# Rows of the loads' sources laid out in DRAM as short pieces with gaps

## The chip, the cores and the metric

The kernel runs on one core of a Trainium2 chip. The time is the device time of one execution in microseconds. The profile is that of one further execution, taken by the hardware profiler. The core has TensorE (PE), VectorE (DVE), ScalarE (ACT), GpSimd (POOL) and SyncE (SP), and 16 DMA engines, which take the loads that SP issues.

## The reference

An mLSTM recurrence (2 batches, 8 heads, 768 steps, head dimension 40) makes 1536 rows of 320 values, and two gated layers of 320 to 2048 to 320 follow:

```python
for t in range(S):
    m_new = np.maximum(f_gate[:, :, t] + m, i_gate[:, :, t])
    f_stab, i_stab = np.exp(f_gate[:, :, t] + m - m_new), np.exp(i_gate[:, :, t] - m_new)
    C = f_stab * C + i_stab * outer(vt, kt)
    n = f_stab * n + i_stab * kt
    y[:, :, t] = sigmoid(o_gate[:, :, t]) * (C @ qt) / np.maximum(np.abs(n @ qt), 1.0)
x = y rearranged to (B * S, H * D)
h = x @ w_in;   x = (h * np.clip(h + 3.0, 0.0, 6.0) / 6.0) @ w_out
h = x @ w2_in;  x = (h * np.tanh(softplus(h))) @ w2_out
```

## The kernel before

The sequence is cut into six chunks of 128 steps. For each chunk the kernel makes scores, decays, a state that is carried on and the chunk's output, which is split into a high and a low part (`x`) and enters layer one. Layer one runs on two chunks of 256 columns first and then on blocks of 512 columns; layer two (`qh`, `bcc`) follows on three blocks of 512.

The weights come as 64-bit floats, in eight slots per layer. A slot of the first matrix (`w1i`, `w2i`) is a tile `ri` of 128 partitions with 6144 bytes each, one of the second (`w1o`, `w2o`) a tile `ro` with 5120 bytes. `narrow` loads such a tile, and ScalarE (the cast to `top`, L364) and VectorE (L366) turn it into 32-bit floats, which are then split into the high and low parts that TensorE uses. `loads` fetches a chunk's q and k as one tile `qke` (8192 bytes per partition) and its k, v and o gate as one tile `kvo` (7744 bytes). `start` and `other_gates` fetch the gates in two parts into `gio`, the first 128 steps and then the other 640; `scan_gates` (L660) is the first to use each part. `constants` fetches `cst`, and the identity matrices go to `eye`. Four of the chunks spread their decays by a store to DRAM (`fzd`, L744) and a load (`fb`, L788) that reads each of 16 rows into 8 partitions.

```python
src = fzd[c].rearrange("a (y r) t -> (a y) (r t)", y=COPIES)
SY.dma_start(out=t["f"], in_=src.unsqueeze(1).to_broadcast([16, 8, R * HL]))
```

Every DMA is issued by SP, in one order for the whole program. That order comes from `Flow`, a planner that runs when the program is built: every piece of work asks for an engine and a time, and a table of priorities and `Flow`'s costs say who gets it. For a load the cost is its number of bytes, which the change leaves as it is. `keep_warm` lets TensorE run a product of zeros (`pz`, L1211) in gaps until the first chunk's output is there. No engine can go past an instruction that waits.

The host lays the arguments out before the launch: `w_in`, `w_out`, `chunks` and `tokens` in `kernel` make the arrays in DRAM, row for row what a partition loads.

Of the kernel before, what the change touches and what calls it, by code (L numbers as in the profile page):

```python
# [12 lines left out]
U16 = mybir.dt.uint16  # L13
# [9 lines left out]
B, H, S, D = 2, 8, 768, 40  # L23
L = 128
NC = S // L
# [12 lines left out]
KVO = B * (2 * DM + H * E1)  # L38
# [262 lines left out]
def mlstm_mlp_kernel(ctx, tc, qk, kvon, gates_io, w1i, w1o, w2i, w2o, eyes, consts, out):  # L301
    nc = tc.nc
    V, A, T, G, SY = nc.vector, nc.scalar, nc.tensor, nc.gpsimd, nc.sync
# [46 lines left out]
    def narrow(src, k, n, name, then):  # L350
        yield in_raw
        size = 4 * k * n
        raw = rpool.tile([128, size + 4], U16, tag="raw", name=f"r{name}")
        loaded = Event()
        yield SP, 256 * size, loaded
        SY.dma_start(out=raw[:, 1 : size + 1].rearrange("p (k s) -> p k s", k=k), in_=src.bitcast(U16))
        yield loaded
        upper = raw[:, 4 : size + 4].rearrange("p (k n s) -> p k n s", k=k, s=4)[:, :, :, 0]
        e = raw[:, 2 : size + 2].bitcast(U32).rearrange("p (k n s) -> p k n s", k=k, s=2)[:, :, :, 0]
        yield in_top  # L360
        top = tops[turn[0] % 2][:, 0 : k * n].rearrange("p (k n) -> p k n", k=k)
        turn[0] += 1
        yield ACT, 0.93 * k * n / 768
        A.copy(top.bitcast(U16).rearrange("p k (n s) -> p k n s", s=2)[:, :, :, 1].bitcast(F16), upper.bitcast(BF16))  # L364
        yield DVE, 0.072 + k * n / 960, True
        V.scalar_tensor_tensor(out=e, in0=e, scalar=13, in1=top,  # L366
                               op0=ALU.logical_shift_right, op1=ALU.bitwise_or)
        flow.put(in_top)
        yield from then(e.bitcast(F32))
        flow.put(in_raw)  # L370
# [4 lines left out]
    def prep(layer, s):  # L375
# [53 lines left out]
        wi, wo = (w2i, w2o) if layer else (w1i, w1o)  # L429
        pi, po = P[f"prep{layer}"][2 * s : 2 * s + 2]  # L430
        a = flow.add(pi, narrow(wi[s], 3, 256, f"i{nm}", split_in))
        b = flow.add(po, narrow(wo[s], 2, DM, f"o{nm}", split_out))
        yield a
        yield b
# [321 lines left out]
    def loads(c, before):  # L756
        t, ev = tiles[c], got[c]
        if before:
            yield before
        if c == 1:  # L760
            flat = xpool.tile([128, 3072], F32, tag="x1", name="qke1")[:, 0 : 16 * L]
            t["qke"] = flat.rearrange("p (b y h t) -> p b y h t", b=B, y=2, h=4)
        else:
            yield in_qke
            t["qke"] = apool.tile([128, B, 2, 4, L], F32, tag="qke", name=f"qke{c}")
        yield SP, 1049e3, ev["qk"], 16, 0.5
        SY.dma_start(out=t["qke"], in_=qk[c])
        t["ring"] = in_x2 if c in (1, 3) else in_kvo
        yield t["ring"]
        kvo = (xpool if c in (1, 3) else apool).tile([128, 3072 if c in (1, 3) else KVO + 256], F32, tag="x2" if c in (1, 3) else "kvo", name=f"kvo{c}")  # L770
        t["tail"] = kvo[:, KVO : KVO + 256]
        t["k"], t["v"], t["o"] = (kvo[:, a:z].rearrange("p (r d) -> p r d", r=R)
                                  for a, z in ((0, R * D), (R * D, KVO - R * D), (KVO - R * D, KVO)))
        yield SP, 992e3, ev["kvo"]
        SY.dma_start(out=kvo[:, 0:KVO], in_=kvon[c * L : (c + 1) * L])

    def gate_loads(c, before):
        t, ev = tiles[c], got[c]
# [515 lines left out]
    with tc.manual_schedule(engines={PE, DVE, ACT, POOL, SP}):  # L1294
# [3 lines left out]
        for c in range(NC):  # L1298
            before = flow.add(P["load"][c], loads(c, before))
# [77 lines left out]
```

## Time and profile before

| what | value |
|---|---|
| time, median of 3 runs | 441.97 us (440.05 to 443.53) |
| profiled execution | 441.46 us, of it a span of 439.4 us |
| PE busy | 422.4 us (96% of the span) |
| DVE, ACT, POOL busy | 302.0, 269.6, 61.8 us |
| DMA packets | 10040, 40.44 MB |

A matmul counts as busy until its modelled end, and the filler product counts too, so PE's share does not tell alone how much of the time is needed. DMA's busy share is a mean over the 16 engines; where it is near 1, transfers wait for one another. The profile's DMA records have a packet's duration; where shares pass 1, neighbouring records overlap. Waits are put down to what ended them, and a wait with no ender in the profile is called "issue".

### The profile page before, as it was taken

How to read it: one execution, taken by the hardware profiler on the slowest of the kernel's cores; microseconds unless marked ns; L12 is line 12 of the kernel's file. 1: busy time of each engine (PE TensorE's matmuls, PEld its weight loads, DVE VectorE, ACT ScalarE, POOL GpSimd, SP SyncE). 2: the span in 40 equal slices, each digit the busy share in tenths (PEclk: the TensorE clock that was granted, in tenths of full speed). 3: DMA queues.
4: the chain of work that ended last, by engine and by line, in shares of the span. 5: the costliest groups of instructions: out<-in, count | busy, mean ns of one | idle time of the engine just before them, and what ended most of it. 6: DMA issues, size and time to landing. Idle time of an engine off the chain costs nothing.

```text
span 439.4 us, 9016 instructions
## 1 busy us (share of the span) xinstructions
PE 422.4 (96%) x3765; PEld 366.5 (83%) x3765; DVE 302.0 (69%) x532; ACT 269.6 (61%) x479; POOL 61.8 (14%) x51
## 2 busy tenths in 40 slices
PE   7869999999999899999998999999999999999996
PEld 5758899999988688887875788999999998989985
DVE  3888999896643953446978537666666666666664
ACT  5547795454544223348976548766676666766665
POOL 2002043213220313313133110000000000000000
PEclk9998999999999999999999999999999999999999
DMA  8976573905003027100755000000010000100001
GB/s 298 400 309 204 176 234 98 343 16 189 1 1 101 3 97 289 68 0 2 272 195 191 2 0 0 1 1 1 0 61 1 1 0 1 45 17 0 1 0 60
DMA packets 10040, 40.44 MB, mean 92 GB/s; under 512 B 2128, under 2 KB 3824, under 8 KB 9232
## 3 DMA queue, kind: packets, MB, share of 16 engines
q1 hardware_dynamic: 10000, 39.87, 25.5%
q8 instruction: 29, 0.48, 0.5%
q14 instruction: 11, 0.09, 0.1%
HBM read 37.64 MB, written 2.23 MB: 91 GB/s over the span
## 4 chain that ended last, share of the span: by engine, by line
PE 64%; DVE 14%; ACT 8%; DMA 8%; issue 3%; POOL 1%; SPq 0%; DVEq 0%; ACTq 0%; POOLq 0%
PE qh L463 18%; PE accw L480 10%; PE phw L463 9%; PE bcc L1180 6%; PE bcc L1179 5%; PE bcc L1178 5%; DMA gio<-in_gates_io 3%; PE acc L480 3%; PE ph L463 2%; DVE fb L842 2%; DMA ri<-in_w2i 2%; DVE c L308 1%; DVE ri L366 1%; DVE kvo L308 1%; ACT top L364 1%
## 5 line engine op out<-in xcount | busy, mean ns | idle before, releaser
L463 PE MATMUL qh<-x,wh 128*128 128x512 f32 x288 | 89.3, 392 | 0.0
L1180 PE MATMUL bcc<-wd,gl 128*128 128x320 f32 x192 | 59.5, 310 | 0.3 <-DVE gl L1135 0.3
L463 PEld LDWEIGHTS qh<-x,wh 128*128 128x128 f32 x288 | 52.3, 188 | 8.7
L1178 PE MATMUL bcc<-wd,gh 128*128 128x320 f32 x192 | 59.4, 309 | 0.0
L1179 PE MATMUL bcc<-wd,gh 128*128 128x320 f32 x192 | 59.3, 309 | 0.0
L463 PE MATMUL phw<-x,wh 128*128 128x512 f32 x192 | 59.2, 394 | 0.0
L1129 DVE SCALAR_TENSOR_TENSOR u<-u,qh 128x512 f32<-128x512 f32 (+1 forms) x49 | 33.1, 675 | 37.6 <-ACT u L1127 37.6
L480 PE MATMUL accw<-ghw,wd 128*128 128x512 f32 x160 | 53.9, 402 | 0.3 <-ACT ghw L550 0.3
L1125 ACT ACTIVATE u<-u,two 128x512 f32<-128x512 f32 (+1 forms) x49 | 35.0, 715 | 30.7 <-DVE u L1123 30.6
L547 DVE SCALAR_TENSOR_TENSOR rw<-rw,phw 128x512 f32<-128x512 f32 x32 | 21.9, 685 | 32.3 <-ACT rw L545 32.1
L463 PEld LDWEIGHTS phw<-x,wh 128*128 128x128 f32 x192 | 35.5, 188 | 7.8
L480 PE MATMUL accw<-glw,wd 128*128 128x512 f32 x96 | 38.3, 399 | 1.6 <-DVE glw L308 1.0
L463 PE MATMUL qh<-x,wl 128*128 128x512 f32 x96 | 37.8, 394 | 0.0
L1178 PEld LDWEIGHTS bcc<-wd,gh 128*128 128x128 f32 x192 | 36.1, 188 | 2.1
L1179 PEld LDWEIGHTS bcc<-wd,gh 128*128 128x128 f32 x192 | 36.1, 188 | 1.9
L1135 DVE SCALAR_TENSOR_TENSOR gl<-u,gh 128x512 fp32r<-128x512 f32 (+1 forms) x49 | 33.1, 675 | 5.6 <-ACT gh L1133 5.4
L1180 PEld LDWEIGHTS bcc<-wd,gl 128*128 128x128 f32 x192 | 36.1, 188 | 0.9 <-DVE gl L1135 0.9
L1119 ACT ACTIVATE u<-qh 128x512 f32<-128x512 f32 (+1 forms) x49 | 28.5, 585 | 12.7 <-PE qh L463 12.6
L545 ACT ACTIVATE rw<-phw,half 128x512 f32<-128x512 f32 x32 | 22.0, 688 | 22.5 <-PE phw L463 22.2
L480 PEld LDWEIGHTS accw<-ghw,wd 128*128 128x128 f32 x160 | 29.4, 188 | 7.6 <-ACT ghw L550 1.2
L463 PE MATMUL ph<-x,wh 128*128 128x256 f32 x192 | 35.1, 290 | 0.1
L1133 ACT ACTIVATE gh<-u 128x512 fp32r<-128x512 f32 (+1 forms) x49 | 30.3, 618 | 6.9 <-DVE u L1129 6.8
(154 smaller groups left out, 836.8 us busy)
## 6 DMA issues: line engine op xcount, KB each, us to landing
ri<-in_w1i SPq DMA_DIRECT2D x8, 768.0 KB, 5.7
qke<-in_qk SPq DMA_DIRECT2D x6, 1024.0 KB, 6.9
ri<-in_w2i SPq DMA_DIRECT2D x8, 768.0 KB, 5.5
kvo<-in_kvon SPq DMA_DIRECT2D x6, 968.0 KB, 7.3
ro<-in_w1o SPq DMA_DIRECT2D x8, 640.0 KB, 7.7
ro<-in_w2o SPq DMA_DIRECT2D x8, 640.0 KB, 4.2
fb<-fzd SPq DMA_DIRECT2D x4, 512.0 KB, 5.9
out<-ot SPq DMA_DIRECT2D x12, 160.0 KB, 1.8
```

Of the source, the lines that this page charges most:

```text
L463: T.matmul(ph, a, b, start=(i == 0), stop=(i == len(seq) - 1))
L480: T.matmul(acc[k], a, b, start=start, stop=stop, skip_group_check=True)
L545: A.activation(r, ph, AF.Relu, bias=half, scale=1.0 / 6.0)
L547: V.scalar_tensor_tensor(out=r, in0=r, scalar=1.0, in1=ph, op0=ALU.min, op1=ALU.mult)
L1119: A.activation(u, ph, AF.Exp)
L1125: A.activation(u, u, AF.Ln, bias=two)
L1129: V.scalar_tensor_tensor(out=u, in0=u, scalar=0.5, in1=ph, op0=ALU.subtract, op1=ALU.mult)
L1133: A.mul(gh, u, -2.0)
L1135: V.scalar_tensor_tensor(out=gl, in0=u, scalar=-2.0, in1=gh.bitcast(F32), op0=ALU.mult, op1=ALU.subtract)
L1178: T.matmul(acc, a, hi, start=st, stop=False)
L1179: T.matmul(acc, a, lo, start=False, stop=False)
L1180: T.matmul(acc, b, hi, start=False, stop=sp)
```

## The change

In DRAM the last axis of seven arrays is cut in pieces, and each piece is followed by a gap of 16 elements (64 bytes of 32-bit values in `qk` and `kvon`, 128 bytes of 64-bit values in the weights). A row of `w1i` or `w2i` was 6144 bytes in one and becomes 3 pieces of 2048, a row of `w1o` or `w2o` was 5120 and becomes 2 of 2560, a row of `qk` was 8192 and becomes 4 of 2048, a row of `kvon` was 7744 and becomes 4 of 1936. The loads take the pieces and leave the gaps out; the tiles in the core's memory are as before, as is everything that reads them.

```diff
@@ narrow
-        SY.dma_start(out=raw[:, 1 : size + 1].rearrange("p (k s) -> p k s", k=k), in_=src.bitcast(U16))
+        SY.dma_start(out=raw[:, 1 : size + 1].rearrange("p (k s) -> p k s", k=k), in_=src[:, :, 0:n].bitcast(U16))
@@ loads
-        SY.dma_start(out=t["qke"], in_=qk[c])
+        SY.dma_start(out=t["qke"].rearrange("p b y h t -> p (b y) (h t)"), in_=qk[c, :, :, 0:512])
...
-        SY.dma_start(out=kvo[:, 0:KVO], in_=kvon[c * L : (c + 1) * L])
+        SY.dma_start(out=kvo[:, 0:KVO].rearrange("p (k s) -> p k s", k=4), in_=kvon[c * L : (c + 1) * L, :, 0 : KVO // 4])
@@ kernel
+    def apart(a):
+        return np.concatenate([a, np.zeros(a.shape[:-1] + (16,), a.dtype)], axis=-1)
...
-        "qk": np.stack([chunks(q), chunks(k)], axis=3),
-        "kvon": np.concatenate([tokens(k), tokens(np.concatenate([v, np.ones_like(v[..., :1])], axis=3)), tokens(o_gate, True)], axis=1),
+        "qk": apart(np.stack([chunks(q), chunks(k)], axis=3).reshape(NC, 128, 4, 512)),
+        "kvon": apart(np.concatenate([tokens(k), tokens(np.concatenate([v, np.ones_like(v[..., :1])], axis=3)), tokens(o_gate, True)], axis=1).reshape(S, 4, -1)),
...
-        "w1i": w_in(moe_w_in[x_order]), "w1o": w_out(moe_w_out), "w2i": w_in(moe2_w_in), "w2o": w_out(moe2_w_out),
+        "w1i": apart(w_in(moe_w_in[x_order])), "w1o": apart(w_out(moe_w_out)), "w2i": apart(w_in(moe2_w_in)), "w2o": apart(w_out(moe2_w_out)),
```

No instruction changes its place on any engine. On SP, the queue of all DMAs, the program begins before as follows (a row has the line, the tile and its source, and the shape of the access; `ri_1` is slot 1 of the first weights):

```order
L356 DMA ri_1_136<-in_w1i 128x3072
L1195 DMA gio<-in_gates_io 16x2x128
L1197 DMA eye<-in_eyes 128x256
L356 DMA ro_0_137<-in_w1o 128x2560
L1251 DMA cst<-in_consts 16x112
L767 DMA qke_103<-in_qk 128x2048
L356 DMA ro_2_138<-in_w1o 128x2560
L775 DMA kvo_153<-in_kvon 128x1936
L356 DMA ri_0_139<-in_w1i 128x3072
L767 DMA qke_155<-in_qk 128x2048
L1255 DMA gio<-in_gates_io 16x2x640
L775 DMA kvo_180<-in_kvon 128x1936
```

And now, on SP at the same place:

```order
L356 DMA ri_1_136<-in_w1i 128x3x1024
L1195 DMA gio<-in_gates_io 16x2x128
L1197 DMA eye<-in_eyes 128x256
L356 DMA ro_0_137<-in_w1o 128x2x1280
L1251 DMA cst<-in_consts 16x112
L767 DMA qke_103<-in_qk 128x4x512
L356 DMA ro_2_138<-in_w1o 128x2x1280
L775 DMA kvo_153<-in_kvon 128x4x484
L356 DMA ri_0_139<-in_w1i 128x3x1024
L767 DMA qke_155<-in_qk 128x4x512
L1255 DMA gio<-in_gates_io 16x2x640
L775 DMA kvo_180<-in_kvon 128x4x484
```

Nothing moved; the loads of weights, `qke` and `kvo` have one axis more.

## Rows read from the trace of the kernel before

**Rows 1.** Stages: length, busy us of each engine, PE clock, DMA share, GB/s

```profile
5.10:21.10 16.00, 13.13 (x257) 9.92 (x258) 13.04 (x26) 10.91 (x24) 0.00 (x0) 1.00 1.00 387
...
29.90:32.10 2.20, 0.04 (x3) 0.07 (x3) 1.51 (x3) 1.39 (x2) 0.00 (x0) 1.00 0.19 67
...
76.70:91.00 14.30, 14.30 (x238) 13.78 (x242) 12.64 (x22) 8.10 (x13) 3.97 (x3) 1.00 0.77 280
91.00:155.00 64.00, 61.64 (x739) 55.08 (x733) 43.66 (x73) 27.24 (x54) 13.56 (x10) 1.00 0.16 51
...
207.00:243.00 36.00, 33.97 (x143) 26.03 (x142) 29.85 (x39) 29.13 (x42) 10.86 (x9) 1.00 0.59 201
243.00:439.00 196.00, 192.36 (x1040) 171.25 (x1038) 125.69 (x213) 132.42 (x224) 3.97 (x3) 1.00 0.03 11
```

**Rows 2.** Chain that ended last, 0 to 32 us: start, length, what

```profile
0.74 4.37 DMA ri<-in_w1i
...
6.25 14.86 DMA gio<-in_gates_io
21.12 0.02 issue
21.14 0.47 DVE mt L660
...
29.89 2.18 issue
```

**Rows 3.** DMA queues, 29.7 to 31 us: packets, MB, share of 16 engines

```profile
q8 instruction: 1, 0.02, 5.1%
```

**Rows 4.** Waits that a DMA ended: us in total, times, longest

```profile
DVE mt L660 <- DMA gio<-in_gates_io: 4.8, 2, 4.5
...
ACT top L364 <- DMA ri<-in_w1i: 3.2, 1, 3.2
...
ACT top L364 <- DMA ri<-in_w2i: 2.4, 2, 2.0
...
DVE fb L842 <- DMA fb<-fzd: 1.6, 1, 1.6
```

**Rows 5.** Chain that ended last, whole span: a later load

```profile
219.91 6.61 DMA ri<-in_w2i
```

**Rows 6.** The page: packets of the queue, and loads, KB, us to landing

```profile
q1 hardware_dynamic: 10000, 39.87, 25.5%
...
ri<-in_w1i SPq DMA_DIRECT2D x8, 768.0 KB, 5.7
qke<-in_qk SPq DMA_DIRECT2D x6, 1024.0 KB, 6.9
...
ro<-in_w1o SPq DMA_DIRECT2D x8, 640.0 KB, 7.7
```

**Rows 7.** DMA queue, 157.2 to 159.1 us, `qke` alone

```profile
q1 hardware_dynamic: 98, 0.80, 99.6%
```

**Rows 8.** DMA queue, 13.9 to 14.9 us, `ri`

```profile
DMA packets 70, 0.43 MB, mean 426 GB/s; under 512 B 1, under 2 KB 1, under 8 KB 70
...
q1 hardware_dynamic: 70, 0.43, 101.3%
```

**Rows 9.** DMA queue, 4.3 to 4.5 us, mostly `eye`

```profile
q1 hardware_dynamic: 67, 0.07, 95.2%
```

**Rows 10.** DMA queue, 168.8 to 169.8 us, `kvo`

```profile
q1 hardware_dynamic: 55, 0.43, 102.1%
```

**Rows 11.** Timeline of SP, 53 to 60 us: start, length, issue

```profile
55.65 0.39 SPq L744 DMA_DIRECT2D fzd<-fz  x1
57.95 0.34 SPq L356 DMA_DIRECT2D ro<-in_w2o  x1
```

**Rows 12.** DMA queue, 139 to 142 us, `fb`

```profile
q1 hardware_dynamic: 198, 0.75, 102.1%
```

**Rows 13.** Stretch from 33.6 to 37 us, columns as in rows 1

```profile
33.60:37.00 3.40, 3.40 (x12) 2.59 (x10) 3.40 (x7) 2.31 (x8) 0.00 (x0) 0.50 0.12 18
```

**Rows 14.** DMA queues, 8 to 21.1 us

```profile
q8 instruction: 1, 0.02, 0.5%
```

## The prediction

> **What bounds the kernel now.** I read the stages first [rows 1]. From 77 us on TensorE is at work nearly all the time: 14.30 of 14.30 us up to 91, 61.64 of 64.00 between 91 and 155, 192.36 of 196.00 after 243. DMA has a share of 0.03 to 0.16 in the last two, so a slower load there costs nothing. The one stage that the loads bound is the start: from 5.1 to 21.1 us the DMA engines have a share of 1.00. TensorE's time there is partly the filler product `pz`, so its busy share says nothing.
>
> The chain of work that ended last [rows 2] shows what the backlog holds up. The first load of `ri` lands at 5.11. The second `gio` load, issued at 6.25, needs 14.86 us, although it is small (16×2×640 floats, 80 KB). It stands behind seven larger loads (`ri`, `ro`, `qke`, `ro`, `kvo`, `ri`, `qke`). VectorE's scan of the gates starts 0.03 us after it. At 29.89 the chain has 2.18 us of "issue", a wait on TensorE that no semaphore explains. In that time one packet of the instruction queue moved [rows 3], and DMA's share over 29.9 to 32.1 is 0.19 [rows 1]: the backlog was just running dry. No row ties the wait to that packet, but a code fetch that came late is the nearest reading.
>
> The waits that a DMA ended [rows 4] are few: 4.8 us of VectorE for `gio`, nearly all of it the first time, before anything is loaded; 3.2 us for the first `ri`; 2.4 us for two loads of `w2i`; 1.6 us for `fb`, whose source is not changed. The later `w2i` wait is on the chain, 6.61 us from issue to use [rows 5], in a stage (207 to 243) where TensorE still works 33.97 of 36.00 us [rows 1].
>
> **The change part by part.** The 44 loads (16 of `ri`, 16 of `ro`, 6 of `qke`, 6 of `kvo`; [rows 6] has the kinds that differ) go in the same order with the same useful bytes. A row of 6144 bytes becomes 3 packets, one of 5120 becomes 2, and the rows of 8192 and 7744 become 4. That is 16×128×2 + 16×128×1 + 12×128×3 = 10,752 packets more, beside 10,000 in the queue now [rows 6]. With 8 of a load's 128 rows on each of 16 engines, an engine gets 16, 8, 24 and 24 more packets per load of weights in, weights out, `qk` and `kvon`.
>
> Price of one more packet. With `qke` alone in flight, 0.996×16×1.9 us over 98 packets is 309 ns for 8192 bytes [rows 7]. A stretch of `ri` gives 1.013×16×1.0 us over 69 data packets and one small write: 234 ns for 6144 [rows 8]. The line through both is 0.0366 ns per byte and 9 ns per packet. Far below on the scale, 67 packets of mostly 1024 bytes (`eye`) average 0.952×16×0.2 us / 67 = 45 ns [rows 9], against 37.5 for the bytes alone: 8 ns left. So short reads stay on the line, and they were sustained back to back. Shares of 101.3% and 102.1% [rows 8, 10] say that records of neighbouring packets overlap by 1 to 2%, 3 to 6 ns of 234 to 297. What a further packet adds to the stream is then 3 to 9 ns; I take **6 ns**.
>
> The backlog: ahead of `gio` each engine gets 16+8+24+8+24+16+24 = 120 more packets, so it lands 0.72 us later (0.36 to 1.08). Behind it come `kvo`, three `ro`, `ri` and `qke`: 24+24+16+24 = 88 more, and the backlog ends 208×6 ns = 1.25 us later (0.6 to 1.9). `gio` is on the chain with 0.03 us to spare, so 0.72 us is paid in full, and TensorE comes to the code fetch that much later. If the fetch goes on starting as the backlog dries up, the wait ends 1.25 us later than now, which is 0.53 us beyond the shift. I count it: **+1.25 us** by 32 us. The other loads of that time (`kvo`, `ro`) move by 0.9 to 1.2 us at their landing while their consumers move by 0.7 to 1.25, so none of them becomes late by more than some tenths. From 77 us on TensorE has little idle time that could take the shift back [rows 1].
>
> Later loads: those of 36 to 91 us meet a DMA share of at most 0.77 (between 76.7 and 91), so a load grows by its own packets and those of one or two neighbours, 0.05 to 0.4 us. No wait for a DMA of that stretch but `fb`'s 1.6 us is on record [rows 4], and TensorE works 14.30 of 14.30 us between 76.7 and 91 [rows 1]; taken as nothing, 0.4 at most. If that cover were gone (a late `ri` at 90 us, with 72 packets more in its queue), that 0.4 us would be the price. The two `w2i` waits grow by 16 to 24 packets each: 0.10 to 0.15 us, of which the one on the chain counts, **+0.15 us**.
>
> SP's issues: a load of one run per row holds SP 0.34 us, the store of `fzd` with two runs per row 0.39 [rows 11]. Each load on the chain could start 0.05 us later; two or three of them make 0.1 us, which I leave inside the range. Queued behind SP's instruction are only further loads. The gap in DRAM itself costs nothing here by the trace: `kvon`'s rows of 7744 bytes start on no multiple of 256 three times in four, and `kvo` still has 1.021×16×1.0 us / 55 = 297 ns [rows 10] where the line says 293, and 55 packets in 16 engine-microseconds is one in 291.
>
> The Trainium skill says otherwise on that last point: "DMA: Bandwidth & Descriptors", section "How a descriptor splits into AXI transactions", lets a read that starts off a 256-byte boundary fetch the bytes below it too. By that, as an estimate, half of the weight pieces would fetch 128 bytes more and most `qk` and `kvon` pieces 100 or so, 3 to 4 ns each; with some 180 pieces ahead of `gio` the sum would be about 0.5 us larger. The `kvo` row does not bear it out.
>
> The sum is 1.25 + 0.15 = **+1.4 us**. The profiled execution took 441.46 us, which gives 442.9; the median of the three runs is 441.97, 0.5 higher, which gives 443.4. I forecast **443.1**. Three runs of the same kernel lie between 440.05 and 443.53, so less than about 1% cannot be told from no change here.
>
> **The rivals.**
> *Short reads are slow, and the start stretches (slower).* One bulk load in the trace already comes from DRAM in packets below 5 KB: `fb`, 4096 bytes, with 198 packets in 3 us at a share of 102.1%: 247 ns each where the line says 159 [rows 12]. That is 1.56 times. If shortness is the reason, all the loads of the start get that factor or more: 16 us before `gio` become 25 or 26, the backlog ends some 15 us later, and with a third hidden by work that has its data the kernel takes about **452**. For it: this is the nearest size and the only long stream of it. Against: `fb` reads the same 16 rows eight times over (L787, L788), the sizes of the weights have no such excess, and `eye` at 1024 bytes has none. It decides from a price of 4.4 us / (208+24 packets) = 19 ns per further packet, three times what I take. The Trainium skill speaks for it ("Perfetto Trace Analysis", "DMA Optimizations"): transfers under 2 KB have significant overhead, and batching them to 4 or 8 KB can dramatically improve throughput. No run so far shows that for a stream of distinct rows.
> *The code fetch gets through earlier (a little faster).* If the fetch near 29.7 us waits its turn among packets, shorter ones hand it over sooner. At best the 2.18 us vanish, against +0.72 from `gio`: −1.5 us, about **440.5**. More would follow if the stretch behind TensorE's idle time with a granted clock of 0.50, or 1.2 GHz (33.6 to 37.0 us) [rows 13], went too: its 3.4 us of matmuls are at most 1.7 at the full clock. That makes about 438.8 at the very best. For it: the wait stands right where the backlog ends. Against: the instruction queue had a packet in the middle of the backlog as well [rows 14].
> *The loads do not come out as short as said.* The tile's side of a weight load is still one run per partition; if a row were moved as before, nothing changes: **442**. Against it: a gap in DRAM leaves no single run to move.
>
> **How the numbers follow.** The forecast's mechanism, some tenths to 2.5 us more, has 0.70; the slow reads 0.17, of which 0.02 stay below 19 ns per packet; the earlier fetch 0.10, of which 0.04 with enough besides (clock, neighbours) to pass 1%; the unchanged packets 0.03. That makes 0.04 faster, 0.79 within 1%, 0.17 slower after giving the forecast's own upper tail 0.02 as well. The range takes in the fetch rival's 440.5 below. Above, the forecast's terms at their upper bounds are 1.9 + 0.4 + 0.15 + 0.1 = 2.6 us on 442 or 444.6 with the runs' scatter of 1.5 on top, and some of the slow rival: **440.5 to 447**.
>
> **What would show it.** After: some 20,750 packets in the queue; `gio` landing near 21.8 us; the 2.18 us of "issue" ending near 33.3; the backlog gone at about 32.9; packets of 2048 bytes at about 84 ns; from 91 us on everything moved by the same 1 to 1.5 us. Wrong would be: packets of 2048 bytes above 97 ns, `gio` after 23.5 us, or a wait for a load of 36 to 91 us that is not in [rows 4].

## The result, and the profile after

The changed kernel takes 445.42 us (median of 16 runs, 442.47 to 448.54); the kernel before took 441.93 us in the same session (16 runs, 439.53 to 443.96). The ratio is 1.0081, 95% interval 1.0056 to 1.0106: **3.5 us slower**, 2.5 to 4.7. The forecast of 443.1 us had the sign and the main place, and its range holds the time, but its +1.4 us is 2.1 us short of the difference. Some executions fall in a slower state, and the ratios leave such runs out, which are two of e6's twelve.

The stages of the changed kernel, columns as in [rows 1]:

```profile
5.10:21.10 16.00, 12.87 (x226) 10.24 (x225) 11.99 (x25) 9.73 (x23) 0.00 (x0) 0.89 1.02 351
...
29.90:32.10 2.20, 2.16 (x77) 2.04 (x69) 2.20 (x7) 0.16 (x1) 0.00 (x0) 1.00 1.04 397
...
155.50:158.94 3.44, 1.90 (x67) 1.65 (x66) 3.30 (x6) 1.29 (x2) 0.71 (x1) 1.00 0.00 0
158.94:162.36 3.42, 3.42 (x43) 2.38 (x41) 0.58 (x2) 0.01 (x1) 1.29 (x1) 0.50 0.69 224
...
243.00:439.00 196.00, 195.67 (x1053) 173.89 (x1052) 127.79 (x216) 135.52 (x227) 4.19 (x3) 1.00 0.04 12
```

In the first line the DMA engines are, on the mean of the stretch, as full as before (1.02), but move 351 GB/s where [rows 1] has 387. Between 29.9 and 32.1 us, where the backlog had run dry (share 0.19 in [rows 1]), it is now in full flow (1.04). At the end TensorE is as busy as before (195.67 of 196.00 us). The two lines in the middle are a stretch at a granted clock of 0.50 (1.2 GHz) behind one with 1.54 us of idle time, which the kernel before did not have at this place.

The chain of work that ended last: start, length, what:

```profile
9.78 13.52 DMA gio<-in_gates_io
23.30 0.02 issue
23.33 0.47 DVE mt L660
...
32.06 2.40 issue
34.46 0.28 PE pf L723 x3
...
60.92 7.49 DMA fb<-fzd
...
158.35 3.17 PE accw L480 x8
```

`gio` lands at 23.30 instead of 21.12 ([rows 2]: 6.25 and 14.86). It is issued 3.5 us later, since SP is held up ahead of it, but stands behind the same loads. The wait called "issue" now runs from 32.06 to 34.46: it has moved by 2.17 us and is 0.22 us longer than in [rows 2]. The eight products at 158.35 take 3.17 us; in the chain of the kernel before, at the same place, they take 2.06.

The page: the queue's packets, MB and share, then loads with KB and median us to landing, as in [rows 6]:

```profile
q1 hardware_dynamic: 20752, 39.87, 26.8%
...
ri<-in_w1i SPq DMA_DIRECT2D x8, 768.0 KB, 6.9
...
ro<-in_w1o SPq DMA_DIRECT2D x8, 640.0 KB, 8.2
```

20,752 packets and the same 39.87 MB: 10,752 more, so the loads did come out as short as the change says.

Waits that a DMA ended, as in [rows 4]:

```profile
DVE mt L660 <- DMA gio<-in_gates_io: 6.0, 2, 5.3
...
ACT top L364 <- DMA ri<-in_w1i: 4.8, 2, 4.0
...
DVE fb L842 <- DMA fb<-fzd: 1.6, 2, 1.4
...
ACT top L364 <- DMA ri<-in_w2i: 1.5, 2, 1.3
...
ACT top L364 <- DMA ro<-in_w1o: 1.2, 1, 1.2
```

The first `ri` lands later (longest wait 4.0 us, 3.2 in [rows 4]), and the wait for a `ro` of the start is twice as long (0.6 us in the kernel before). One wait is new: 0.8 of the 4.8 us for `ri` are spent at 94.4 us, on the load issued at 87.65. The waits for `w2i` did not grow; 0.5 us for a `ro` of `w2o` came in.

Where the shift builds up can be read by pairing VectorE's 653 instructions, which stand in the same order in both kernels, by number. How much later than before they start (us), by the place in the kernel before:

```
place (us)      21.1   32.5   59.5   65.3   104.6  144.8  158.2  206.6  244.2  end
after          +2.19  +2.40  +2.37  +3.11  +3.15  +3.36  +4.86  +4.84  +4.31  +4.37
```

There are three steps: **+2.40 us at the start**, +0.74 at the first wait for `fb`, +1.50 at 158 us, where the clock is at 0.50; 0.5 come back between 207 and 244. Between the steps the line is flat to 0.05 us, but for 0.2 between 104.6 and 144.8: up to 207 us nothing takes a shift back, and the new wait at 94.4 us adds 0.04. These are two executions, 4.4 us apart, where the medians are 3.5 us apart.

### The profile page after: what moved, and what is told of

It is laid out like the page before. It is cut to its first block, busy times and chain, and to the rows that moved or that the text cites. A ratio compares the mean times of both kernels' runs of the same rounds, so it can differ in the third digit from the quotient of the medians.

```text
span 443.7 us, 9016 instructions
## 1 busy us (share of the span) xinstructions
PE 425.6 (96%) x3765; PEld 369.2 (83%) x3765; DVE 303.5 (68%) x532; ACT 270.0 (61%) x479; POOL 60.9 (14%) x51
## 2 busy tenths in 40 slices
DMA packets 20792, 40.44 MB, mean 91 GB/s; under 512 B 2128, under 2 KB 6896, under 8 KB 20752
## 3 DMA queue, kind: packets, MB, share of 16 engines
q1 hardware_dynamic: 20752, 39.87, 26.8%
## 4 chain that ended last, share of the span: by engine, by line
PE 62%; DVE 13%; DMA 11%; ACT 7%; issue 3%; SPq 2%; POOL 1%; ACTq 0%; DVEq 0%; POOLq 0%
PE qh L463 17%; PE accw L480 10%; PE phw L463 8%; PE bcc L1180 6%; PE bcc L1179 5%; PE bcc L1178 5%; DMA fb<-fzd 4%; DMA gio<-in_gates_io 3%; PE acc L480 3%; PE ph L463 2%; DVE fb L842 2%; DVE c L308 1%; DMA ro<-in_w2o 1%; DMA ri<-in_w2i 1%; DMA fzd<-fz 1%
## 5 line engine op out<-in xcount | busy, mean ns | idle before, releaser
L1180 PE MATMUL bcc<-wd,gl 128*128 128x320 f32 x192 | 59.5, 310 | 0.3 <-DVE gl L1135 0.3
L1178 PEld LDWEIGHTS bcc<-wd,gh 128*128 128x128 f32 x192 | 36.1, 188 | 2.1
L1179 PEld LDWEIGHTS bcc<-wd,gh 128*128 128x128 f32 x192 | 36.1, 188 | 1.9
L1180 PEld LDWEIGHTS bcc<-wd,gl 128*128 128x128 f32 x192 | 36.1, 188 | 0.9 <-DVE gl L1135 0.9
L545 ACT ACTIVATE rw<-phw,half 128x512 f32<-128x512 f32 x32 | 22.1, 690 | 22.3 <-PE phw L463 21.9
```

Source lines behind the costliest of these rows:

```text
L545: A.activation(r, ph, AF.Relu, bias=half, scale=1.0 / 6.0)
L1178: T.matmul(acc, a, hi, start=st, stop=False)
L1179: T.matmul(acc, a, lo, start=False, stop=False)
L1180: T.matmul(acc, b, hi, start=False, stop=sp)
```

## The experiments

The theory after the result: the start's backlog is late by more than its packets' price of 6 ns, and the end follows it. Against it stood that the later loads pay a good part; that it is the gap, not the shortness; that the cost comes with each load rather than with each packet; that all of it passes through `gio`; and that TensorE's clock takes a part. All ratios are against the kernel before, run beside the experiment (medians of 441.4 to 441.9), with 95% intervals.

**e1, e2: only the 13 loads issued before 32 us in pieces, or only the other 31.** Whole and cut copies of the arrays lie side by side in DRAM, and each load picks one:

```diff
+def short(*load):
+    return load in EARLY
...
-        a = flow.add(pi, narrow(wi[s], 3, 256, f"i{nm}", split_in))
+        a = flow.add(pi, narrow(wi[s] if short("i", layer, s) else (w2iw if layer else w1iw)[s], 3, 256, f"i{nm}", split_in))
```

and the same for `ro`, `qke` and `kvo`; e2 has `not in EARLY`. Expected of e1:

> Only the 13 loads issued before 32 us are in short pieces, the other 31 are whole rows. Theory A (the start pays: the first load comes late and the backlog stretches, gio lands 2.2 us later, and that shift stays): gio again near 23.3 us, time at least 2.5 of the 3.5 us slower than before, 1.0055 to 1.008. Theory B (each later load, 0.35 us slower to its first packet, pays a share as well): at most 2 of the 3.5 us, 1.0025 to 1.0045.

Measured: 443.81 us (12 runs), ratio 1.0039 (1.0019 to 1.0058). Expected of e2:

> The 13 loads of the start are whole rows, the 31 later ones in short pieces. Theory A: gio near 21.1 us and the time within 1 us of before, 0.999 to 1.002. Theory B: 1.5 us or more slower, 1.0035 to 1.005, with the fb load of 58 us and the casts at 85 to 95 and 212 to 235 us later.

Measured: 443.07 us (12 runs), ratio 1.0028 (1.0005 to 1.0052). In e1's profile `gio` lands at 23.32 and the backlog ends at 35.02, as in the changed kernel (23.30 and 34.95); in e2's at 20.48 and 32.22 (21.12 and 32.23 before). The start alone is worth +0.39%, 1.7 us. That is in Theory B's range, and Theory A's 1.0055 is missed. The later loads come out at +0.28%, 1.2 us, between the two theories and just clear of noise. Both together are 0.67%, which agrees with 0.81% within the intervals. Where the later loads lose it the profile of e2 does not show; that execution even ended 0.7 us ahead of the one of the kernel before. What it does show is that each of them starts late, see e8.

**e3: the gap alone.** Every row in one piece, with the gap only at its end:

```diff
-        SY.dma_start(out=t["qke"].rearrange("p b y h t -> p (b y) (h t)"), in_=qk[c, :, :, 0:512])
+        SY.dma_start(out=t["qke"].rearrange("p b y h t -> p (b y h t)"), in_=qk[c, :, 0:2048])
```

(`ri`, `ro`, `kvo` alike.)

> Every row is moved in one piece as before, and only the gap at its end is there, so that most rows start off a multiple of 256 bytes. Theory A and B alike (the number of pieces is what costs): packets of 6144 bytes at 234 ns, gio near 21.1 us, ratio 0.998 to 1.002. Rival C (where a read starts is what costs): packets longer by 3 to 4 ns, gio 0.2 us later, and if the gap carried the change, a ratio near 1.008.

Measured: 442.82 us (12 runs), ratio 1.0011 (0.9987 to 1.0035): no change clear of noise, and not the 1.008 of Rival C. DMA queue of e3, `qke` alone between 158.7 and 160.5 us, then `kvo` between 171.8 and 172.8:

```profile
q1 hardware_dynamic: 94, 0.77, 101.2%
...
q1 hardware_dynamic: 55, 0.43, 101.9%
```

1.012×16×1.8 us / 94 = 310 ns for 8192 bytes, 309 in [rows 7]; 1.019×16×1.0 us / 55 = 296 ns for 7744, 297 in [rows 10]. The rows of `qke` now lie 8256 bytes apart, so most of them start on no multiple of 256 bytes. The Trainium skill, "DMA: Bandwidth & Descriptors", section "How a descriptor splits into AXI transactions", would have these reads fetch more; no such cost shows here.

**e4 and e8: pieces of half the size, and every row in two pieces.** If the price is one per packet, it is proportional to their number. In e4 pieces have 968 to 1280 bytes, in e8 2560 to 4096:

```diff
-        SY.dma_start(out=raw[:, 1 : size + 1].rearrange("p (k s) -> p k s", k=k), in_=src[:, :, 0:n].bitcast(U16))
+        SY.dma_start(out=raw[:, 1 : size + 1].rearrange("p (k s) -> p k s", k=2 * k), in_=src[:, :, 0 : n // 2].bitcast(U16))
```

(e8 has `k=2` and `0 : k * n // 2`; the other loads and the arrays go with it.)

> Pieces of half the size, 968 to 1280 bytes. By the line of 9 ns per packet plus 0.0366 ns per byte a piece of 1024 bytes takes 46 to 47 ns; an engine gets 312 more packets than before ahead of gio in place of 120... worked out as 40+24+56+24+56+40+56 = 296. Theory A with a price that goes by the piece (2.2 us for 120): gio 5 us later than before, near 26 us, time 8 to 9 us slower, 1.017 to 1.021. If the late first packet is the larger part and goes by the number of descriptors (0.4 us for 256 more in a load): first packet of the first load 1 us later than before, SP's instruction 0.9 us instead of 0.54. Rival: the pieces overlap and the price is 3 ns: gio only 1 us later than in the changed kernel, 1.010 to 1.012.

> Every row in two pieces (2560 to 4096 bytes): 56 more packets per engine ahead of gio than before, in place of 120. Theory P (each further packet costs 9 to 10 ns of the stream): backlog from the first landing to the third qke 1.0 us longer than before (28.1 us in place of 27.1; the changed kernel 29.0), gio near 22.3. Theory F (a load in pieces costs its 0.15 us by being in pieces, however many): the same 29 us as the changed kernel, gio near 23.2. Either way the first packet of a load alone comes 0.35 us later, if it goes by the form of the access; a third of that if it goes by the number of packets.

Measured: e4 445.9 us (6 runs), ratio 1.0095 (1.0059 to 1.0131); e8 443.0 us (12 runs), ratio 1.0032 (1.0013 to 1.0051). Against the kernel before, an engine has by the end of the backlog 104 further packets in e8, 208 in the changed kernel and 520 in e4, at +1.4, +3.5 and +4.2 us. It is not proportional. `gio` lands at 21.47 us in e8 and at 22.93 in e4, against 23.30 in the changed kernel: e4, with two and a half times the further packets, is earlier, and far from the 26 us expected of a price by the piece; e8 is below the 22.3 expected at 9 to 10 ns. How the stream itself behaves is read between 10 and 21.1 us, where the engines have a share of 1.00 or more in each of these kernels. The DMA queue there of the kernel before, of e8, of the changed kernel and of e4 (packets, MB, share of 16 engines):

```profile
q1 hardware_dynamic: 736, 4.40, 100.4%
```

```profile
q1 hardware_dynamic: 1317, 4.30, 102.3%
```

```profile
q1 hardware_dynamic: 2104, 4.19, 104.1%
```

```profile
q1 hardware_dynamic: 3718, 3.82, 108.5%
```

Without the cut, the changed kernel's 4.19 MB would take 11.1×4.19/4.40 = 10.57 us and 701 packets. The 1403 further packets, 88 on each engine, cost 0.53 us: **6.0 ns each**. For e4 the same working gives 1.46 us over 192 packets, 7.6 ns; for e8, 0.25 us over 37, 6.8 ns. The other kernels whose early rows are whole move 4.37 to 4.39 MB there (e2, e3, e10), so each of these figures is good to a nanosecond or two. In a full queue the price per packet is thus 5 to 8 ns, and the rest of the delay has to come from elsewhere.

It comes from before 10 us. DMA queue between 0.7 and 10 us, the same four kernels:

```profile
q1 hardware_dynamic: 698, 2.87, 86.0%
```

```profile
q1 hardware_dynamic: 1058, 2.68, 81.9%
```

```profile
q1 hardware_dynamic: 1254, 2.33, 81.3%
```

```profile
q1 hardware_dynamic: 2507, 2.59, 86.9%
```

The changed kernel is 0.54 MB behind by then, which is 1.36 us at 4.40 MB in 11.1 us; e8 is 0.19 MB behind and e4 0.28. With early rows whole the scatter is 0.1 MB (2.77 to 2.87 in the kernel before, e2, e3 and e10); e1 and e9, cut there like the changed kernel, have 2.34 and 2.46. Of the 1.36 us, 43 further packets per engine make 0.26 at 6 ns, and the start of the first load makes another part (below). Some 0.7 us are left, and they arise between 6.2 and 10 us: the changed kernel moves 1.04 MB there (e1 and e7 1.06, e9 1.22), the kernel before 1.38, e8 1.42 and e4 1.31. The DMA engines' share is 0.87 from 6.2 to 8 us and 0.93 from 8 to 10, while SP is held by the loads of `ri` and `qke` (below). Neither the number of packets nor the pieces as such explain it, for e4 and e8 do not lose it. Its cause is open.

SP's timeline, the changed kernel, with start, length and load:

```profile
0.74 0.67 SPq L356 DMA_DIRECT2D ri<-in_w1i  x1
...
6.24 1.60 SPq L356 DMA_DIRECT2D ri<-in_w1i  x1
7.88 1.86 SPq L767 DMA_DIRECT2D qke<-in_qk  x1
9.78 2.46 SPq L1255 DMA_DIRECT2D gio<-in_gates_io  x1
...
60.32 0.55 SPq L356 DMA_DIRECT2D ro<-in_w2o  x1
```

and of e8:

```profile
59.02 0.54 SPq L356 DMA_DIRECT2D ro<-in_w2o  x1
```

The same `ro` holds SP 0.34 us in [rows 11]. It is 0.54 in e8 and 0.55 in the changed kernel, with two pieces per row in both, and it is 0.54 us as well in e4, with four. The first packet is late by more than that. A `qke` load into an empty queue, in stretches of the columns of [rows 1]: the kernel before (issued at 155.09),

```profile
155.09:156.05 0.96, 0.96 (x5) 0.78 (x6) 0.96 (x3) 0.51 (x1) 0.38 (x1) 1.00 0.00 0
156.05:157.00 0.95, 0.95 (x7) 0.49 (x5) 0.11 (x1) 0.00 (x0) 0.92 (x1) 1.00 0.79 138
```

e8 (issued at 155.68),

```profile
156.63:157.00 0.37, 0.37 (x3) 0.30 (x2) 0.12 (x1) 0.00 (x0) 0.37 (x1) 1.00 0.00 0
157.00:157.60 0.60, 0.60 (x7) 0.21 (x5) 0.00 (x0) 0.00 (x0) 0.56 (x1) 1.00 0.97 123
```

and the changed kernel (issued at 158.45):

```profile
159.40:159.77 0.37, 0.37 (x2) 0.28 (x2) 0.12 (x1) 0.00 (x0) 0.37 (x1) 0.50 0.00 0
159.77:160.40 0.63, 0.63 (x3) 0.51 (x2) 0.00 (x0) 0.00 (x0) 0.55 (x1) 0.50 0.78 111
```

Up to 0.96 us behind the issue nothing moves in any of them. Then the whole rows come at once, and the cut ones 0.36 us later, whether in two pieces or four (DMA share 0.00 in the stretch of 0.37 us). In e4, with eight, it is again 1.32 us from issue to first packet; in e3, with a gap and whole rows, 0.96. The other late loads that meet an empty queue agree in all twelve traces: 0.95 to 1.03 us with whole rows, 1.32 to 1.40 with rows in pieces. **So a load whose rows come in several runs costs a fixed third of a microsecond at its start, whatever the number of runs**, beside the price per packet. It counts for the first load and for each late one that meets an empty queue; that a full queue hides it is likely and not shown.

**e7: the changed kernel with its first load whole.** The edit is `short` as in e1, with `return load != ("i", 0, 1)`: only the first load of `ri` takes the whole copy.

> The changed kernel, with only the first load of all (ri, slot 1) as whole rows. Theory A1 (of the 2.2 us at gio, 0.5 to 0.8 come from the first load, whose first packet starts 0.4 us later): first load lands near 5.1, gio near 22.6 us, time 0.5 us below the changed kernel, 1.005 to 1.008. Rival A2 (the late first load is made good in the backlog, since the queue behind it only gets fuller): gio again near 23.3.

Measured: 444.58 us (12 runs), ratio 1.0061 (1.0038 to 1.0084). The first `ri` lands at 5.07 instead of 5.92, as before the change, `gio` at 22.68 instead of 23.30, the backlog's end at 34.35 instead of 34.95. e1 and e9, with the first load cut, have `gio` at 23.32 and 23.20. So 0.6 of the 2.18 us that `gio` is late come from the first load's start, as Theory A1 had it. In this execution, the slowest of e7's twelve, the gain is lost again by 32.5 us, where VectorE is 3.84 us late (table below): TensorE was granted a clock of 0.50 from 22.9 to 39.9 us. The times lie 0.2% apart, in the right direction, and their intervals overlap.

**e5, e6: the gates out of the backlog.** 752 of the 768 steps go with the first small `gio` load, ahead of all weights; e5 does it to the changed kernel, e6 to the one before:

```diff
-        SY.dma_start(out=gio[:, :, 0:L], in_=gates_io[:, :, 0:L])
+        SY.dma_start(out=gio[:, :, 0 : S - 16], in_=gates_io[:, :, 0 : S - 16])
...
-        SY.dma_start(out=gio[:, :, L:], in_=gates_io[:, :, L:])
+        SY.dma_start(out=gio[:, :, S - 16 :], in_=gates_io[:, :, S - 16 :])
```

> The changed kernel, with 752 of the 768 steps of the gates in the first gio load and only 16 in the second. Theory A (the shift of the start reaches TensorE through the second gio load): VectorE's second scan no longer waits near 23 us but starts where its engine gets to it, before 21 us; the wait called issue still ends near 34.5 us if it hangs on the end of the backlog, and then the time gains at most 1 us on the changed kernel, 1.004 to 1.007. Rival D (gio alone is what makes the start late, and the rest follows from it): all of the 2 us of the start come back, 1.001 to 1.004.

> The kernel before with the same move of the gates, as the control for the run before this one. Theory A: issue still ends near 32 us, ratio 0.997 to 1.000. Rival D: the scan gains 1 to 2 us and so does the time, 0.994 to 0.997. The difference of the two runs is then what short pieces cost by other ways than the second gio load: about 2.5 us by A, 1 us by D.

Measured: e5 444.5 us (6 runs), ratio 1.0075 (1.0046 to 1.0104); e6 442.53 us (12 runs), ratio 0.9999 (0.9968 to 1.0030). The distance stays 0.76%. That `gio` alone carries the start's delay to the end, as the prediction had it and Rival D has it here, is refuted. The scan did not start before 21 us, as expected, but at 22.82. The chain of e5 shows what takes `gio`'s place:

```profile
15.81 0.80 DVE ro L366
...
20.28 0.90 DVE ri L366
21.20 0.91 ACT wh L404
...
22.82 0.39 DVE mt L660
...
31.62 2.01 issue
```

The casts of the loads `ro` and `ri` now stand on the chain ahead of the scan. They do so in e6 as well and at nearly the same times, the cast of `ri` at 20.15 and the scan at 22.76 us, so up to there the two executions do not differ. They part at the "issue" wait, which runs from 31.62 to 33.63 us in e5 and from 31.56 to 32.59 in e6. By which of the late loads the shift reaches TensorE once `gio` is off the path is therefore not shown. With whole rows `gio` is not always the one that is waited for either: in e2, e3 and e10 the scan starts 0.05 to 0.8 us after `gio` has landed, straight behind other work of VectorE (`wl`).

**e9, e10: products that fill TensorE's idle time.** In the changed kernel's profile TensorE is at 0.50 three times behind idle time, from 12.2, 36.1 and 158.9 us on; in the one before once, [rows 13]. Here products that nothing reads fill two idle places, in the changed kernel (e9) and in the one before (e10):

```diff
+        for _ in range(0 if c else 8):
+            T.matmul(pf[:, 0:128], ident, ident, start=True, stop=True, skip_group_check=True)
         T.transpose(pf[:16, 0:128], g[:, 0:16], ident)
...
+        for _ in range(6 if c == 4 else 0):
+            T.matmul(x[1][:, 0:128], ident, ident, start=True, stop=True, skip_group_check=True)
```

> The loads in pieces, as in the changed kernel, and in two of TensorE's idle stretches (before the transposes of the first gates, idle 2.36 us up to 11.88; ahead of the last chunk's cross products, idle 1.54 us up to 157.22) 8 and 6 products of the identity with itself that nothing reads; no idle time before a needed instruction is used up by design. If part of the change's price is paid through TensorE's clock, since its idle stretches fell so that the granted clock dropped to 0.50 behind them: the stretches at 0.50 behind these two places (12.17 to 15.58 and 158.94 to 162.36 in the changed kernel's profile) are gone, the eight products at 158.35 take about 2.1 us again and not 3.17, the mean granted clock over the runs rises from 0.987 to 0.989 or more, and the median falls to about 443.5 to 444.5. If the clock only accompanies the time: the mean clock may rise, but the median stays at 445 to 446, or rises by the few tenths that the products cost.

> The control: the same products in the kernel with whole loads. Its idle stretches there are 1.85 us up to 11.09 and 1.54 us up to 153.87, so the products fit. Its profile has no stretch at 0.50 behind either place, its mean granted clock is 0.990 over its runs. If the clock carries a part of the price: little to win here, the median 441 to 442, and the distance from the kernel with pieces and the same products shrinks from 0.8% to 0.5% or so. If not: the median as without the products and the distance stays 0.8%.

Measured: e9 445.4 us (6 runs), ratio 1.0096 (1.0059 to 1.0132); e10 441.49 us (12 runs), ratio 1.0001 (0.9977 to 1.0024). Stretches of e9, columns as in [rows 1]:

```profile
12.85:16.30 3.45, 3.45 (x131) 3.05 (x128) 2.64 (x7) 1.24 (x3) 0.00 (x0) 1.00 1.05 397
155.50:158.94 3.44, 3.21 (x76) 2.74 (x75) 3.30 (x7) 0.77 (x2) 0.62 (x2) 1.00 0.02 5
158.94:162.36 3.42, 3.42 (x74) 2.66 (x74) 1.31 (x6) 0.00 (x0) 0.84 (x1) 1.00 0.87 277
```

Both places have the full clock (1.00), and the step of 1.5 us at 158 is gone: e9's instructions are 2.80 us late at 144.8 and 2.81 at 158.2. Another stretch at 0.50 came in e9, from 24.3 to 31.1 us, behind 1.64 us of idle time. The mean granted clock over the runs rose from 0.9868 to 0.9897, as expected. The time did not fall. The clock as a carrier of the 3.5 us finds no support; the two ratios' intervals put e9 between 0.3% below and 0.6% above the changed kernel, so a gain of up to 1.3 us is not excluded. Nor did the products level the two kernels' clocks, for e10's mean rose as well, to 0.9940. The single runs help here. At a mean clock of 0.992 or more the changed kernel's three runs average 442.7 us and the 31 runs of the kernel before that stood beside the experiments 441.2; between 0.986 and 0.991 it is 445.6 (7 runs) against 442.0 (27), below that 445.9 (6) against 442.6 (16). At like clock a distance of 1.5 to 3.6 us stays.

The two runs show something else. TensorE's timeline of e10 around its "issue" wait:

```profile
31.61 0.77 PE L842 MATMUL fb<-identz,ist 128*64 128x64 f32 x11 [2.91 <-issue]
32.31 0.53 PE L721 MATMUL pf<-dd,cst 16*104 16x16 f32 x2
32.68 0.57 PE L723 MATMUL pf<-eye,pr 16*128 16x8 f32 x2
33.18 0.38 PE L725 MATMUL pf<-eye,pr 16*64 16x8 f32 x4
```

In the changed kernel (chain above: `pf` L723 x3, which is L725 here) and in the one before the wait stands behind the first of those last four passes. In e10, and at the same pass in e9, it stands 11+2+2+1 = 16 passes earlier, and the eight products added ahead of it are 16 passes. So the wait belongs to a fixed count of instructions from the program's start, whatever they are, which speaks for the loading of TensorE's code and against a load of data. The packets of the instruction queue say the same. Its third one starts at 29.74 us in the kernel before and at 32.02 in the changed kernel, and the wait ends 2.3 and 2.4 us later; in all eleven traces that have the wait it is 2.2 to 2.7 us. It is not the backlog's end as such that ends the wait: in e6 the backlog is over at 31.04 us, the packet starts at 30.17, and the wait ends at 32.59. In e7, where TensorE comes to this place only at 36 us, there is no wait. What sets the packet's time is not shown.

How late VectorE's instructions are in one execution each, worked out as above:

```
place (us)      21.1   32.5   59.5   65.3   144.8  158.2  244.2  end
e3             +0.65  +0.61  +0.94  +1.49  +1.49  +3.00  +2.84  +2.82
e10            -0.39  +1.22  +2.34  +2.32  +2.32  +2.32  +1.18  +1.21
e8             +0.79  +1.17  +1.06  +1.05  +0.59  +0.59  +0.57  +0.63
e1             +2.63  +2.84  +2.84  +3.38  +3.37  +3.38  +2.43  +2.45
e9             +2.35  +3.36  +2.28  +2.81  +2.80  +2.81  +3.64  +3.62
e4             +2.73  +3.45  +3.78  +4.31  +4.78  +6.29  +7.61  +7.67
e2             -0.49  -0.31  -0.27  +0.28  -0.42  -0.41  -0.73  -0.67
e7             +1.57  +3.84  +4.34  +4.87  +4.88  +6.40  +5.96  +6.02
e5             +1.60  +1.56  +1.91  +2.45  +1.75  +3.26  +2.62  +2.68
e6             +1.54  +0.52  -0.54  -0.55  -1.24  -1.24  -2.93  -2.88
```

The step at 158 appears in e3 too, whose loads are whole and whose time is that of the kernel before, and so does one of 0.55 us between 59.5 and 65.3. e10, whole as well, is 2.3 us late from 40 us on, by a longer "issue" wait (2.91 us) and a stretch at 0.50 behind it, though it is ahead at 21.1. Such steps come with the execution more than with the change; that is why the medians decide, and a profile only says where.

## Why the prediction was right, and where it fell short

- **What bounds the kernel**: borne out for the start. The largest step arises in the first 32 us, and 2.40 us at 32.5 are 2.37 at 59.5.
- **Packets and bytes, and no cost of the gap**: right, 20,752 packets, and e3 with its 310 and 296 ns.
- **Price of one more packet, 6 ns**: right. It is 6.0 ns in the changed kernel's full queue between 10 and 21.1 us, 6.8 in e8 and 7.6 in e4. The packets themselves came out as forecast too: 1.022×16×1.8 us / 347 = 85 ns for 2048 bytes (last section), where the prediction had 84.
- **"SP's issues: Each load on the chain could start 0.05 us later"**: the step that failed. It was sized by a store with two runs per row (0.39 us, [rows 11]), which is an operation of the other direction. A load of several runs holds SP 0.54 us and has its first packet 0.36 us later than a whole one. For the first load, on which everything waits, e7 puts this at 0.6 us of `gio`'s delay. With 120 packets at 6 ns that is 1.3 of 2.18 us. The other 0.9 us had no term in the sum: some 0.7 of it arise between 6.2 and 10 us, where the changed kernel's stream is slower than in e8 or e4, and why is open.
- **The backlog's end**: +2.72 us instead of +1.25: `gio`'s 2.18, and 0.54 us for the 88 packets behind it, 6 ns each as forecast. The 32.9 us named as its end does not go with the +1.25: the last load of the backlog landed at 32.23 in the kernel before.
- **"`gio` is on the chain with 0.03 us to spare"**: true of that chain, though the first of the seven loads named ahead of `gio` had landed (5.11) before `gio` was issued (6.25). But `gio` is not the only carrier. With the gates loaded early (e5 against e6) the difference in time stays. Other work of VectorE comes to the scan at about the same time, so that in e2, e3 and e10, with whole rows, the scan waits for that and not for `gio`; a chain shows one of several paths of about equal length.
- **The "issue" wait follows the backlog's end**: right for the changed kernel in direction. It ends at 34.46 (33.3 forecast), and in e1, with the same backlog, at 34.90. What it follows, in all eleven traces that have it, is a packet of the instruction queue, 2.2 to 2.7 us ahead; in e6 it ends 1.55 us after the backlog. That it is a code fetch was a guess in the prediction; the place of the wait in e9 and e10 and this packet bear it out. The rival of an earlier fetch is out: the wait did not shrink.
- **"Later loads … taken as nothing"**: too low, as far as the noise lets one say. At most 0.4 us, 0.1%, was allowed; e2 has +0.28% (0.05 to 0.52), and the changed kernel against e1 some 0.4% (0.1 to 0.7). The late start of each load, 0.36 us, is the shown difference; which waits turn it into time is not shown. The `w2i` term of +0.15 us is not seen either: those waits total 1.5 us, less than the 2.4 of [rows 4].
- **The signs of being wrong**: one of the three came, a wait for a load of 36 to 91 us that is not in [rows 4]. It is the 0.8 us at 94.4 us, and it shifted nothing by more than 0.04 us in this execution. `gio` at 23.30 stayed just short of the 23.5 named, and 85 ns for 2048 bytes well short of 97.
- **Short reads slow like `fb`**: refuted for price and size; e4 with pieces of about 1 KB has 7.6 ns per packet where the rival needed 19. e8 reads `qke` in packets of the size of `fb`'s, 4096 bytes, at 1.016×16×1.8 us / 184 = 159 ns, where `fb` takes 247 [rows 12]. The rule in the Trainium skill that spoke for it, "Perfetto Trace Analysis", section "DMA Optimizations", holds in its direction: between 10 and 21.1 us the stream moves 4.40 MB in long packets, 4.19 at about 2 KB, 3.82 at about 1 KB, so batching wins 5 to 15% of the rate there.
- **The range, 440.5 to 447**: it holds 445.4, but not by its mechanism. The terms at their upper bounds made +2.6 us, and +3.5 was measured; the range reached higher because the runs' scatter and a part of the slow rival had been added. That was luck as far as the mechanism goes.

By size: the start is +2.4 us in the profile and 1.7 us (0.8 to 2.6) by e1; the later loads 1.2 us (0.2 to 2.3) by e2. Together that is 2.9 of the 3.5 us, and within the intervals all of it; a part by TensorE's clock is neither needed nor excluded.

## What to carry to other kernels

A load is priced in two parts: so many nanoseconds per packet in a full queue (here 5 to 8), and a fixed part at its start that depends on its form, which counts wherever the queue is empty, above all for the first load. Where a chain goes through one late load of a backlog, ask what else is ready at about the same time: moving that one load off won nothing here. A price read from a stretch of a trace holds only if the engines are full in all of it; from 8 us on, two microseconds earlier, the changed kernel's stream (2404 packets and 4.79 MB in 13.1 us, 861 and 5.17 before) would make it 9.6 ns here. And an operation of the other direction, such as a store here, is no measure for a load's issue.

## What the runs showed of the hardware

- The time from issue to first packet is 0.96 us for a load of one run per row and 1.32 us for one of two, four or eight, and SP is held 0.33 and 0.54 us.
- `qke` alone in the queue, in 1.8 us that begin some 0.9 us after the load's first packet in each. The DMA queue there of the kernel before (8192 bytes), of e8 (4096), of the changed kernel (2048) and of e4 (1024):

```profile
q1 hardware_dynamic: 93, 0.76, 99.8%
```

```profile
q1 hardware_dynamic: 184, 0.75, 101.6%
```

```profile
q1 hardware_dynamic: 347, 0.71, 102.2%
```

```profile
q1 hardware_dynamic: 670, 0.69, 108.7%
```

  The rate falls with the number of pieces, by 1, 7 and 9%, in a load by itself as in the full queue.
- SP is held while the queue is full: 1.60, 1.86 and 2.46 us for single loads of the changed kernel, and in e4 longer yet:

```profile
6.45 4.18 SPq L356 DMA_DIRECT2D ri<-in_w1i  x1
```

  In e4 the DMA engines stay full meanwhile (a share of 1.07 from 6.2 to 8 us and 1.05 from 8 to 10). In the changed kernel they do not (0.87 and 0.93), so whether it costs anything there is open.
- TensorE's wait near 32 us sits at a fixed number of instructions: with eight products more ahead of it, which are 16 passes, it comes 16 passes earlier in the program. It ends 2.2 to 2.7 us after a packet of the instruction queue starts, in all eleven traces that have it.
- The granted clock of TensorE falls to 0.50 behind idle stretches in some executions and not in others: the same 1.54 us of idle time ahead of the products at 158 us led to it in the changed kernel and not in the kernel before. It shifts one execution by about 1.5 us and should not be read as a change's effect from a single profile.
